# Moving one finish, one scan and one block of transposes at the head of the second up stage

## Chip, cores and metric

The kernel runs on one core of a Trainium2 chip. The metric is the device time of one execution in microseconds (us); the median of four runs before the change is 380.81 us, from 380.46 to 381.58.

## What is computed

The reference is a gated linear attention followed by a feed-forward block with a SoLU activation and a layer norm. All data are float32 on the core.

```python
# attention: batch 4, heads 8, sequence 768, head_dim 48
for t in range(S):
    state = alpha[:, :, t, :, None] * state + einsum('bhd,bhe->bhde', k[:, :, t], v[:, :, t])
    y[:, :, t] = einsum('bhd,bhde->bhe', q[:, :, t], state)
x = y.transpose(0, 2, 1, 3).reshape(3072, 384)
# feed-forward: 384 -> 1024 -> 384
h = x @ w_in
solu = h * softmax(h)
ln = (solu - mean) / sqrt(var + 1e-6) * g_ln
out = ln @ w_out
```

## The kernel before

**Tiling.** The sequence of 768 is cut into six groups of 128 tokens (numbered 0 to 5), each for all four batches. Attention is done in chunked form: within a group, queries and keys are scaled by products of alpha, a masked score matrix is multiplied by the values, and what lies before the group is carried in a state. Scaled queries and keys need running products along the tokens, which VectorE (DVE) makes with scans. The 48 entries of a head are kept as a first 32 and a last 16 (two heads' last entries share a block of 32 rows), so that there are three parts of four blocks each: scan parts 0 and 1 for the first 32 entries, part 2 for the last 16.

**An up stage.** For a group g the loop at the end of `fast_path` (line 891 on) takes the eight pieces f = 0 to 7 of the 1024 hidden columns. `up` issues six matmuls into a PSUM bank h (line 389; there are two such banks), then `up_act`: ScalarE's exponential e (line 403), DVE's product u = h * e (line 404, which frees the bank) and ScalarE's square of u (line 405). `running` (line 420) adds e on GpSimd (POOL) and the square on DVE to running sums, from the second piece on. A `down` stage multiplies u by w_out for one chunk, that is, one batch of a group (line 500), in two halves.

**finish** (lines 511 to 540) closes a chunk. On DVE it issues four instructions: it copies one column of sums (L523), makes two small one-column results (L525, L528), and for group 0 adds a multiple of `mean_sb` to the down result (L533). POOL takes a power (L537), ScalarE scales the row block into `o_sb` (L539), and SyncE (SP) stores it (L540).

**What attention does meanwhile.** While group g is in its up stage, attention of group g+1 is prepared. An order written by hand, the tables `usual` and `first` (lines 828 to 839), names for each piece s what is issued at the head, behind the up, in the middle and at the tail; `attend` (line 841) carries it out. Each engine works in program order. `first` holds for g = 1, the stage which is called the second up here. Names that matter:

- `scan_on(g, i)` (line 229): the forward scan of part i on DVE, aT <- aT, seed (L222). For i = 2 a reciprocal (L233) writes the seeds of all parts first. "on0" and "on1" in the table are parts 0 and 1.
- "lasts" (lines 199 and 251): one DVE transpose of the queries' last 16 entries into qe (L200), and one POOL multiply by scan part 2 (L254).
- "firsts" (lines 196 and 251): one larger DVE transpose into qv (L197), then two POOL multiplies by scan parts 0 and 1 (L254), then the load of the next queries on SP (L141).
- "apart": two ScalarE copies of qe into qv (L247), one for even heads and one for odd.
- "states": the key-value products on TensorE (PE, L364) and four adds to the state on DVE (L374). "v" loads the values on SP (L179). "decay": multiplies of the state on POOL (L263, L264).
- "keys_back": twelve transposes on PE (L300) and three ScalarE copies (kg, L302).
- "scores0" and "scores1": 64 matmuls each into four PSUM banks (L281). "masked0" and "masked1": four DVE products each, which empty those banks into sT (L292). "read0" to "read3" and "values" multiply state and values (L315) into the same four banks.
- "alpha": transposes of alpha and `alpha_over` on ScalarE (L214). `keys` are two POOL multiplies of kT (L243).

**Just ahead of the second up** the program is written out: scans of group 2's alpha backward, `keys_T(2)`, `keys(2)`, load of keys, `scan_on(2, 2)`, `read_values(1)`, `alpha_over(2)`, load of alpha, the rest of `down(3)`, and `finish(3)` (line 824). The loop has a variable `after` (line 899): a chunk in it is finished behind the next piece's `up`.

Of the kernel before, what the change touches and what calls it, by code (L numbers as in the profile page):

```python
# [32 lines left out]
def fast_path(ctx, tc, q, k, v, alpha, moe_w_in, moe_w_out, moe_g_ln, out):  # L33
# [13 lines left out]
    B, H, S, D = q.shape  # L47
# [90 lines left out]
    def load(src, dst, g):  # L138
        t = slice(g * P, (g + 1) * P)
        for b in range(B):  # L140
            nc.sync.dma_start(  # L141
                out=dst[32 * b : 32 * b + 32].rearrange("t h u d -> t h (u d)"),
                in_=src[b, :, t, :].rearrange("h (t u) d -> t h (u d)", u=TQ),
            )
# [65 lines left out]
    def alpha_over(g):  # L210
        x = an.rearrange("p h u d -> p (h u d)")
        sq = one.tile([P, 768], FP, name="sq").bitcast(U8)[:, 0 : x.shape[1]]
        for i, sign in enumerate((1.0, -1.0)):
            nc.scalar.activation(  # L214
                out=sq, in_=x, func=AF.Relu, scale=sign, bias=mone, accum_out=over[:, g, i : i + 1]
            )

    def scan(out, data, start, flip):
        a, o, s = (x.rearrange("p j s -> p (j s)") for x in (data, out, start))
        if flip:  # L220
            a, o, s = a[:, ::-1], o[:, ::-1], s[:, ::-1]
        nc.vector.tensor_tensor_scan(out=o, data0=a, data1=s, initial=1.0, op0=ALU.mult, op1=ALU.add)  # L222
# [6 lines left out]
    def scan_on(g, i):  # L229
        part = slice(NP * i, NP * i + NP)  # L230
        if i == 2:

            nc.vector.reciprocal(out=seed[:, :, 0:1], in_=h4[:, :, 1:2])  # L233
            nc.scalar.copy(out=fend[:, g], in_=h4[:, :, 1])
        scan(aT[:, part], aT[:, part], seed[:, part], False)
# [77 lines left out]
    def y_mm(b, a, r, row, lhsT, rhs, stop=False):  # L313
        begun = reading["begun"]
        nc.tensor.matmul(  # L315
            y_bank(b)[quarter(r), a], lhsT=lhsT, rhs=rhs, start=(b, r) not in begun, stop=stop,
            tile_position=(row, 32 * r), skip_group_check=True,
        )
        begun.add((b, r))
# [23 lines left out]
    def read_values(g, batches=range(B)):  # L343
        if 0 in batches:
            gr[g]["x"] = pair.tile([P, KC, B, P], FP, name="x")
        for b in batches:
            for n, part in enumerate(parts):
                for a, r, h, e in part:
                    y_mm(b, a, r, 0, vn[:, b, h, e], sT[:, b, h], n == len(parts) - 1)
        for b in batches:  # L350
            nc.scalar.copy(out=gr[g]["x"][:, :, b], in_=reading["y"][b])
# [29 lines left out]
    def up(g, f):  # L381
        up_mm(g, f)
        up_act(g, f)
# [110 lines left out]
    def down(n, half, part=slice(0, HF)):  # L494
        g, b = divmod(n, B)
        d = st[n]
        if half == 0 and part.start == 0:
            d["o"] = ps_o.tile([P, 512], FP, tag="o", name="o")
        for f in range(half * HF + part.start, half * HF + part.stop):
            nc.tensor.matmul(  # L500
                d["o"][:, 0 : DM + 1], lhsT=u_of(g, f)[:, b * P : b * P + P], rhs=w_out[:, f], start=(f == 0),
                stop=(f == FC - 1), skip_group_check=True,
            )
# [7 lines left out]
    def finish(n):  # L511
        g, b = divmod(n, B)
        d = st[n]
        s, o = sums[:, n], d["o"][:, 0:DM]
        t0 = b * S + g * P
        if g == G - 1:
            o_sb = work.tile([P, DM], FP, name="o_sb")
            r = gr[g]["r"][:, b : b + 1]
            nc.scalar.activation(out=o_sb, in_=o, func=AF.Copy, scale=r)
            nc.scalar.dma_start(out=out[t0 : t0 + P, :], in_=o_sb)  # L520
            d.clear()
            return
        nc.vector.tensor_copy(out=s[:, 0:1], in_=d["o"][:, DM : DM + 1])  # L523
        t = small.tile([P, 1], FP, name="t")
        nc.vector.scalar_tensor_tensor(  # L525
            out=t, in0=s[:, 0:1], scalar=-1.0 / DFF, in1=s[:, 0:1], op0=ALU.mult, op1=ALU.mult
        )
        nc.vector.tensor_tensor(out=s[:, 3:4], in0=t, in1=gr[g]["s"][:, b : b + 1], op=ALU.add)  # L528
        if g == 0:

            if not d.get("moved"):
                o = work.tile([P, DM + 1], FP, name="o_mean")[:, 0:DM]
            nc.vector.scalar_tensor_tensor(  # L533
                out=o, in0=mean_sb, scalar=s[:, 0:1], in1=d["o"][:, 0:DM], op0=ALU.mult, op1=ALU.add
            )
        r = small.tile([P, 1], FP, name="r")
        nc.gpsimd.tensor_tensor(out=r, in0=s[:, 3:4], in1=mhalf, op=ALU.pow)  # L537
        o_sb = work.tile([P, DM], FP, name="o_sb")
        nc.scalar.activation(out=o_sb, in_=o, func=AF.Copy, scale=r)  # L539
        nc.sync.dma_start(out=out[t0 : t0 + P, :], in_=o_sb)  # L540
        d.clear()
# [272 lines left out]
    for i in range(3):  # L814
# [2 lines left out]
    keys(2)  # L817
    load(k, kn, 3)
    scan_on(2, 2)
    read_values(1)  # L820
    alpha_over(2)
    load(alpha, an, 3)
    down(3, 1, slice(3, HF))
    finish(3)

# [2 lines left out]
        behind={0: "states v keys", 1: "load on2 on0 on1", 2: "lasts firsts", 3: "apart", 5: "decay", 6: "alpha", 7: "back"},  # L830
# [2 lines left out]
    )  # L833
    first = dict(
        head={3: "keys_back", 5: "masked0", 6: "masked1"},
        behind={0: "states v", 1: "on0 on1", 2: "lasts firsts", 3: "apart", 5: "decay", 7: "alpha back"},
        tail={4: "scores0", 5: "scores1", 6: "begin read0 read1"},
        middle={7: "read2 read3 values"},
    )
# [1 line left out]
    def attend(a, what):  # L841

        more = a + 1 < G
        if what == "v":
            load_v(a)
        elif what == "keys":
            keys_T(a)
            keys(a)
            if more:
                load(k, kn, a + 1)  # L850
        elif what[:2] == "on":
            scan_on(a, int(what[2]))
        elif what == "lasts":
            lasts(qn, qe)
            queries(2)
        elif what == "firsts":
            firsts(qn, qv[:, 0:H])
            queries(0)
            queries(1)
            if more:  # L860
                load(q, qn, a + 1)
        elif what == "apart":
            apart()
        elif what == "decay":
            decay(a)
        elif what == "keys_back" and more:
            keys_back(a)
        elif what[:6] == "scores":
            scores(a, int(what[6]))
        elif what[:6] == "masked":  # L870
            masked(int(what[6]))
        elif what == "alpha" and more:
            alpha_T(a + 1)
            alpha_over(a + 1)
        elif what == "load" and more:
            load(alpha, an, a + 1)
        elif what == "back" and more:
            for i in range(3):
                scan_back(a + 1, i)
        elif what == "begin":  # L880
            read_begin()
        elif what[:4] == "read":
            read_state(int(what[4]))
        elif what == "values":
            read_values(a)
        elif what == "states":
            next_state(a - 1)
# [3 lines left out]
    for g in range(1, G + 1):  # L891
        rise, att = g < G, g + 1 < G
        plan = first if g == 1 else usual

        def at(where, s):
            for what in plan[where].get(s, "").split() if att else ():
                attend(g + 1, what)

        after = None
        if not rise:  # L900
            break
        for s in range(FC):
            at("head", s)
            if rise:
                up(g, s)
            if after is not None:
                finish(after)
                after = None
            if s == 0 and g > 1:
                token_sums(g - 1)  # L910
            at("behind", s)
            for f in centres.get(s, ()) if g == 1 else ():
                centre(f)
            if rise and s:
                running(g, s)
            at("middle", s)
            if rise and s == FC - 1:
                todo.append((g * B, 0))
            step = todo.pop(0)
            if step:  # L920
                n, half = step
                down(n, half)
                if half:
                    after = n
            at("tail", s)
        if after is not None:
            finish(after)
        todo = [(n, half) for n in range(g * B, g * B + B) for half in range(2)][1:]
# [492 lines left out]
```

## Time and profile before

| what | value |
| --- | --- |
| median of four runs | 380.81 us (380.46 to 381.58) |
| profiled execution, its own time | 380.86 us |
| its span, first to last instruction | 379.0 us, granted TensorE clock 0.998 |
| PE matmuls busy | 365.9 us |
| VectorE, ScalarE, GpSimd busy | 244.0, 146.9, 128.4 us |
| PE busy in 100 to 120 us, in 120 to 140 us | 18.78, 19.27 us |
| PE busy in each later stretch of 20 or 40 us up to 360 us | all of it |

All times within the execution are microseconds from the start of the span. The profiler's span is 1.86 us shorter than the execution's own time; what lies around it is taken as fixed. A timeline row gives start, length, engine, line of the kernel, operation, output <- inputs, shape and count; what stands in brackets is the time that the engine sat idle before the row and what released it. A row's length runs until its result is written, so the next row of an engine can begin a little before the end of the one ahead of it; it also holds time in which the instruction was started and could not go on. A chain row gives start, length and what the end of the execution waited for at that time. "issue" is time in which the profile shows no wait.

### The profile page before, as it was taken

Reading aid. Unit: us, or ns where it says so; the run is one execution under the profiler, and the core shown is the slowest. Engines: PE = TensorE matmul, PEld = TensorE weight load, DVE = VectorE, ACT = ScalarE, POOL = GpSimd, SP = SyncE. Lnnn points to the kernel's source line nnn. Section 1 sums busy time; section 2 is a strip of 40 time slices with the busy share of each in tenths; the row PEclk is TensorE's granted clock in tenths of the full one; section 3 lists DMA queues with packets and bytes.
Section 4 is the critical chain, followed back from the end, with each engine's and each line's share of the span. In section 5 each row is a group of like instructions: output and inputs, shape, how many; then the busy total and the mean of one; then the engine's idle time right before and its main releaser. Section 6 shows DMA issues by size and latency. Waiting matters only on the chain.

```text
span 379.0 us, 10523 instructions
## 1 busy us (share of the span) xinstructions
PE 365.9 (97%) x4659; PEld 219.8 (58%) x4659; DVE 244.0 (64%) x379; ACT 146.9 (39%) x263; POOL 128.4 (34%) x134
## 2 busy tenths in 40 slices
PE   8789999999898999999999999999999999999995
PEld 8675355566654575555575555675556675555552
DVE  1988879988988876874665874665875411455410
ACT  3628774593455252225351224451233131233111
POOL 5040000042145980662630671630672420333210
PEclk9999999999999999999999999999999999999999
DMA  9983989304096001950002950002400000000011
GB/s 187 192 307 110 222 267 154 85 0 128 24 221 133 3 7 27 186 144 21 22 25 39 202 115 22 23 24 46 62 0 22 22 24 2 22 21 21 22 44 49
DMA packets 65526, 30.78 MB, mean 81 GB/s; under 512 B 47032, under 2 KB 63680, under 8 KB 65472
## 3 DMA queue, kind: packets, MB, share of 16 engines
q1 hardware_dynamic: 64448, 29.10, 34.6%
q10 hardware_dynamic: 1024, 0.92, 0.8%
q8 instruction: 38, 0.62, 0.7%
q14 instruction: 16, 0.13, 0.1%
HBM read 25.30 MB, written 4.72 MB: 79 GB/s over the span
## 4 chain that ended last, share of the span: by engine, by line
PE 71%; DVE 13%; SPq 5%; DMA 5%; ACT 2%; issue 2%; POOL 0%; DVEq 0%
PE o L500 30%; PE h L389 26%; PE y L315 7%; PE a L281 5%; SPq L153 3%; DMA room<-in_moe_w_in_dram 2%; DVE hT L222 2%; DMA out_dram<-o_sb 2%; PE kv L364 1%; DMA an<-in_alpha_dram 1%; DVE sT L292 1%; DVE aT L197 1%; SPq L189 1%; DVE room L404 1%; DVE low L610 1%
## 5 line engine op out<-in xcount | busy, mean ns | idle before, releaser
L500 PE MATMUL o<-w_out,room 128*128 128x385 f32 x384 | 133.8, 491 | 0.0
L389 PE MATMUL h<-x,w_in 128*128 128x512 f32 x288 | 132.4, 599 | 0.6 <-DVE room L404 0.5
L500 PEld LDWEIGHTS o<-w_out,room 128*128 128x128 f32 x384 | 71.2, 190 | 55.8 <-issue 13.1
L389 PEld LDWEIGHTS h<-x,w_in 128*128 128x128 f32 x288 | 52.8, 189 | 59.7 <-issue 48.4
L404 DVE TENSOR_TENSOR room<-h,e 128x512 f32<-128x512 f32 x40 | 27.6, 689 | 81.8 <-ACT e L403 81.7
L403 ACT ACTIVATE e<-h 128x512 f32<-128x512 f32 x40 | 23.9, 598 | 107.4 <-PE h L389 107.4
L420 POOL TENSOR_TENSOR p<-p,e 128x512 f32<-128x512 f32 x30 | 41.9, 1395 | 15.7 <-ACT e L403 15.6
L537 POOL TENSOR_TENSOR r<-sums,mhalf 128x1 f32<-128x1 f32 x20 | 14.9, 746 | 78.6 <-DVE sums L528 78.5
L405 ACT ACTIVATE u<-room 128x512 f32<-128x512 f32 x40 | 25.2, 631 | 36.8 <-DVE room L404 36.8
L292 DVE TENSOR_TENSOR sT<-a,mask 128x512 f32<-128x512 f32 x42 | 26.1, 682 | 8.3 <-PE a L281 8.2
L263 POOL TENSOR_TENSOR state<-state,hT 128x192 f32<-128x192 f32 x20 | 11.3, 582 | 53.4 <-DVE hT L222 53.4
L243 POOL TENSOR_TENSOR kT<-kT,hT 128x1024 f32<-128x1024 f32 (+1 forms) x8 | 14.2, 1792 | 42.0 <-DVE kT L197 33.7
L222 DVE TENSOR_TENSOR_SCAN hT<-aT,unit 128x516 f32<-128x516 f32 x18 | 23.2, 1355 | 7.5 <-ACT aT L683 7.5
L420 DVE TENSOR_TENSOR p<-p,u 128x512 f32<-128x512 f32 x30 | 23.0, 767 | 6.5 <-ACT u L405 6.5
L281 PEld LDWEIGHTS a<-qv,kT 32*128 32x128 f32 x704 | 21.9, 186 | 8.7 <-issue 2.4
L281 PE MATMUL a<-qv,kT 32*128 32x128 f32 x704 | 24.7, 278 | 1.9 <-POOL qv L254 1.1
L222 DVE TENSOR_TENSOR_SCAN aT<-aT,seed 128x516 f32<-128x516 f32 x18 | 26.3, 1493 | 0.2
L315 PE MATMUL y<-sT,vn 128*32 128x128 f32 x768 | 23.6, 274 | 2.7 <-issue 2.3
L315 PEld LDWEIGHTS y<-sT,vn 128*32 128x32 f32 x768 | 20.9, 110 | 4.9 <-issue 3.9
L214 ACT ACTIVATE sq<-an,mone 128x1536 uint8<-128x1536 f32 x12 | 18.9, 1572 | 0.2
L315 PE MATMUL y<-qv,state 32*32 32x128 f32 x960 | 16.7, 277 | 0.0
L539 ACT ACTIVATE o_sb<-o,r 128x384 f32<-128x384 f32 x16 | 9.3, 581 | 18.8 <-POOL r L537 18.8
(146 smaller groups left out, 371.6 us busy)
## 6 DMA issues: line engine op xcount, KB each, us to landing
an<-in_alpha_dram SPq DMA_DIRECT2D x20, 192.0 KB, 4.2
vn<-in_v_dram SPq DMA_DIRECT2D x10, 384.0 KB, 6.2
out_dram<-o_sb SPq DMA_DIRECT2D x20, 192.0 KB, 1.9
room<-in_moe_w_in_dram SPq DMA_DIRECT2D x6, 512.0 KB, 8.5
room<-in_moe_w_out_dram SPq DMA_DIRECT2D x8, 384.0 KB, 4.2
kn<-in_k_dram SPq DMA_DIRECT2D x16, 192.0 KB, 4.6
qn<-in_q_dram SPq DMA_DIRECT2D x16, 192.0 KB, 3.7
kn<-in_k_dram SPq DMA_DIRECT2D x4, 384.0 KB, 5.8
```

What stands on the lines that cost most here:

```text
L214: nc.scalar.activation(out=sq, in_=x, func=AF.Relu, scale=sign, bias=mone, accum_out=over[:, g, i : i + 1])
L222: nc.vector.tensor_tensor_scan(out=o, data0=a, data1=s, initial=1.0, op0=ALU.mult, op1=ALU.add)
L281: nc.tensor.matmul(a[b][:, i], lhsT=kT[quarter(b), kb], rhs=qv[quarter(b), qb], start=kb == h, stop=kb != h, tile_position=(32 * b, 0), sk ...
L292: nc.vector.tensor_tensor(out=sT[:, b, half * NP : half * NP + NP], in0=a[b], in1=mask[:, None, :].to_broadcast([P, NP, P]), op=ALU.mult,)
L315: nc.tensor.matmul(y_bank(b)[quarter(r), a], lhsT=lhsT, rhs=rhs, start=(b, r) not in begun, stop=stop, tile_position=(row, 32 * r), skip_g ...
L389: nc.tensor.matmul(h, lhsT=w_in[:, a, f * P : (f + 1) * P], rhs=d["x"][:, a].rearrange("p b t -> p (b t)"), start=(a == 0), stop=(a == KC ...
L403: nc.scalar.activation(out=e, in_=h, func=AF.Exp)
L404: nc.vector.tensor_tensor(out=u, in0=h, in1=e, op=ALU.mult)
L405: nc.scalar.activation(out=u2, in_=u, func=AF.Square)
L420: eng.tensor_tensor(out=p, in0=d[0][i] if f == 1 else p, in1=d[f][i], op=ALU.add)
L500: nc.tensor.matmul(d["o"][:, 0 : DM + 1], lhsT=u_of(g, f)[:, b * P : b * P + P], rhs=w_out[:, f], start=(f == 0), stop=(f == FC - 1), skip ...
L537: nc.gpsimd.tensor_tensor(out=r, in0=s[:, 3:4], in1=mhalf, op=ALU.pow)
```

## The change

Three edits, all in the order of instructions. `finish(3)` is no longer issued ahead of the loop but, through `after = B - 1`, behind the first piece's `up` of the second up stage. Its place ahead of the loop is not taken; forward scan part 0 of group 2 is issued directly behind part 2 instead of behind the second piece. In `first`, "lasts" moves from behind piece 2 to behind piece 1, ahead of scan part 1; "firsts" stays behind piece 2.

```diff
@@ -817,11 +817,11 @@
     keys(2)
     load(k, kn, 3)
     scan_on(2, 2)
+    scan_on(2, 0)
     read_values(1)
     alpha_over(2)
     load(alpha, an, 3)
     down(3, 1, slice(3, HF))
-    finish(3)
@@ -833,7 +833,7 @@
     first = dict(
         head={3: "keys_back", 5: "masked0", 6: "masked1"},
-        behind={0: "states v", 1: "on0 on1", 2: "lasts firsts", 3: "apart", 5: "decay", 7: "alpha back"},
+        behind={0: "states v", 1: "lasts on1", 2: "firsts", 3: "apart", 5: "decay", 7: "alpha back"},
         tail={4: "scores0", 5: "scores1", 6: "begin read0 read1"},
         middle={7: "read2 read3 values"},
     )
@@ -896,7 +896,7 @@
-        after = None
+        after = B - 1 if g == 1 else None
         if not rise:
             break
```

On DVE the order from scan part 2 on becomes: scan 0, u of piece 0, the finish's four, the four state adds, u of piece 1, lasts, scan 1, the first running sum, u of piece 2, firsts, the second running sum, u of piece 3. Before, it was: the finish's four, u of piece 0, the state adds, u of piece 1, scan 0, scan 1, the first running sum, u of piece 2, lasts, firsts, the second running sum, u of piece 3. On ScalarE the exponential and the square of piece 0 come ahead of `o_sb`, which stays ahead of the exponential of piece 1. On POOL the multiply of qe comes ahead of the first running sum. PE and SP keep their orders.

## Prediction

> **What bounds the kernel now.** The page comes first: who is busy, and for how much of the span.
>
> ```profile
> PE 365.9 (97%) x4659; PEld 219.8 (58%) x4659; DVE 244.0 (64%) x379; ACT 146.9 (39%) x263; POOL 128.4 (34%) x134
> ```
>
> PE sets the time, but its 97% holds stalls inside groups of matmuls. The busy time by stretches of 20 us gives PE 18.78 in 100 to 120, 19.27 in 120 to 140, and all of every stretch from 140 to 360. So this change can gain only before 130 us; what moves PE there moves the end by as much. PE's own timeline of that place, second up, shows it (last columns: length, operation, count, idle time before and its releaser):
>
> ```profile
> 113.71 5.32 PE L389 MATMUL h<-x,w_in 128*128 128x512 f32 x12
> 120.17 0.50 PE L281 MATMUL a<-qv,kT 32*128 32x128 f32 x8 [1.15 <-POOL qv L254]
> 121.01 2.01 PE L281 MATMUL a<-qv,kT 32*128 32x128 f32 x56 [0.33 <-ACT qv L247]
> ...
> 125.72 3.60 PE L281 MATMUL a<-qv,kT 32*128 32x128 f32 x64
> ```
>
> The first scores (L281) wait for the queries, and the second scores take 3.60 where the same 64 matmuls take 2.00 in the chain at 174.08: 1.60 us of hidden wait. The chain that ended last, followed back from there, names what they wait for:
>
> ```profile
> 115.59 1.07 DVE qe L200
> 116.66 1.91 DVE qv L197
> 118.57 0.52 DVE p L420
> 119.09 0.61 DVE room L404
> ...
> 119.72 0.63 ACT u L405
> 120.35 1.22 ACT qv L247 x2
> 121.57 0.49 ACT e L403
> ...
> 123.47 1.36 DVE p L420
> 124.83 2.40 DVE sT L292 x4
> ...
> 127.28 2.05 PE a L281 x58
> ```
>
> Read upwards: the second scores need the banks that masked0 (L292) empties; masked0 stands on DVE behind u4's running sum (p), that behind Square 4, exp 4, the two apart copies (L247), Square 3 and u3 (119.09). I write uN, exp N for chunk N of this up. So the change is worth what it does to u3 and to that last sum.
>
> At the start of the stage ScalarE is late and DVE idles for it. ScalarE's timeline, then DVE's:
>
> ```profile
> 107.84 0.61 ACT L539 ACTIVATE o_sb<-o_mean,r 128x384 f32<-128x384 f32 x1 [2.25 <-POOL r L537]
> 108.36 0.58 ACT L403 ACTIVATE e<-h 128x512 f32<-128x512 f32 x1
> ```
> ```profile
> 103.59 2.40 DVE L222 TENSOR_TENSOR_SCAN aT<-aT,seed 128x516 f32<-128x516 f32 x1
> ...
> 106.07 0.92 DVE L525 SCALAR_TENSOR_TENSOR t<-sums 128x1 f32<-128x1 f32 x1
> ...
> 108.97 0.69 DVE L404 TENSOR_TENSOR room<-h,e 128x512 f32<-128x512 f32 x1 [1.27 <-ACT e L403]
> ```
>
> ScalarE is free at 105.6 (alpha_over's last row, 105.40 + 0.19) but stands 2.25 us before the fourth chunk's o_sb; exp 0 is behind it, though h is ready at about 105.2. DVE then idles 1.27 before u0.
>
> One more thing prices the change. Some DVE operations stretch beside POOL: the scan at 103.59 took 2.40 and the one-column operation at 106.07 took 0.92, against 1.20 for the scan at 160.04 and a median of 0.16 for L525. POOL's two key multiplies run from 102.72 to 104.90 and from 104.86 to 106.97. The scan ends 1.1 after the first one ends, the small operation ends with the second. Operations with two operands in SBUF take turns between the engines. u (L404), which reads h from PSUM, took 0.69 beside POOL too. Who is next when both wait is shown one stage on, in the timelines of DVE and POOL:
>
> ```profile
> 157.87 2.25 DVE L222 TENSOR_TENSOR_SCAN aT<-aT,seed 128x516 f32<-128x516 f32 x1
> 157.16 1.86 POOL L420 TENSOR_TENSOR p<-e 128x512 f32<-128x512 f32 x1
> ```
>
> POOL asked at 157.16, during a scan of 156.72 to 157.87; it ended at 159.02, 1.15 later, and only then did the next scan, queued right behind the first, run. The one that waits gets its turn before the other's next instruction.
>
> **The change, step by step.** No instruction is added or removed; orders change on DVE, ScalarE and POOL, none on PE and SyncE (the listing of both orders). Lengths on DVE are start to start from its timeline: u 0.61 (108.97 to 109.58), four state adds 1.27 (109.58 to 110.85), scan 1.13 (160.04 to 161.16), sum p 0.6, lasts 0.96 and firsts 1.91 (115.51, 116.47, 118.38); the finish's four about 1.05 without POOL.
>
> 1. Scan 0 ahead of u0. DVE is free of scan 2 at 105.9, as now. The second key multiply has waited since 104.86 and takes its turn to 106.97; scan 0 runs to 108.05. It fills the idle 1.27, but 1.05 of that is a wait: the gap is not free room.
> 2. Exp 0 runs at 105.6, u0 at 108.05 (now 108.97). PE's third up waits for u0 now (0.24, row at 109.72); that wait goes, worth nothing by itself, since PE waits at 119 anyway.
> 3. The finish behind it: DVE 108.65 to 109.7, power on POOL 109.25 to 109.80, o_sb 109.83. Exp 1 is still behind o_sb: 110.35, ending 110.93. State adds 109.7 to 110.8. u1 at 110.96, now 110.85. All that step 2 gained is spent here. The store goes out some 2 us later and load_v behind it on SyncE by as much: issued at about 111 instead of 108.95, over 5.0 us as now, landing a median of 6.2 after issue, so by 123; values need it at 138.04: hidden. Nothing else waits there: q's load needs the queries (118.60).
> 4. Lasts a block sooner: 111.57 to 112.7; POOL asks for the qe multiply at about 112.85. Scan 1 is dispatched at 112.54, so it is first, to 113.65; qe (1.18, row at 116.81) then to 114.82, and the sum p of DVE, which is ready at 113.65, waits 1.15 and runs to 115.4. u2 at 115.39, now 114.91: **0.48 later**. Before, no sum met qe, which ran beside the transposes.
> 5. Firsts directly behind u2: 115.99 to 117.90, now 116.47 to 118.38: 0.48 sooner, as 0.96 of lasts is gone from here. The next sum ends at 118.48.
> 6. ScalarE: Square 2 (116.09), three kg copies and exp 3 follow u2 at once now (115.63, 116.16, 117.58), so exp 3 moves with it, to 118.05 to 118.67. u3 needs both and starts at 118.70, now 118.98: **0.28 sooner**. The old order had 0.78 of slack between exp 3's end (118.20) and u3; the new one has none, so exp 3 is what is late next.
> 7. Square 3, apart, exp 4, u4, Square 4: each 0.28 sooner; u4's sum is ready at 123.19 (now 123.47). POOL's two query multiplies end at about 119.65 and 120.8 (now 120.12 and 121.26), its sums at 122.5 and 123.8 (now 122.93 and 124.28). The sum waits for the last of these and starts at 123.8 instead of 124.28. Masked0 starts 0.43 to 0.48 sooner.
> 8. PE: the first scores end with apart, 0.28 sooner; the second with masked0, **0.43 sooner**. Behind them up6, the state reads and masked1 keep their distances: the decay on POOL follows the same sums, and its end (131.18) is 0.84 before the reads (132.02). From there PE has no wait that the chain shows, so the end moves by 0.43. PE's ceiling here is 119.0 to 129.25 less 2.00 + 2.77 + 2.00, or 3.5 us; the change gets an eighth of it.
>
> Sum: 380.86 (the profiled execution's own time, span 379.0) less 0.43 is 380.4. The execution is 0.05 above the median of the four, 380.81; I leave that in the range.
>
> The Trainium skill (SBUF — State Buffer, "Who interferes with whom") says that a DVE instruction with two SBUF inputs contends with a GpSimd instruction that reads SBUF, exclusively, and that the first to issue blocks the other. The rows above (2.40 against 1.20) agree, and it speaks against this change, which moves a scan and a POOL multiply next to each other. Without it, steps 1 and 4 would lose no 1.05 and 1.15, and the estimate would be about 378.7; with it, 380.4. Who is next when both wait that section does not say.
>
> **Rivals.** (a) *The turns fall for the change.* If DVE keeps its turn between scans 2 and 0, all to u3 is some 0.75 sooner (u1 is then bound by exp 1 behind o_sb); if scan 1's sum goes ahead of qe, u2 is 1.15 sooner. Either gives 0.43 + 0.75 or 0.43 + 1.15, so 379.7 to 379.3, both together 378.5. Against it: the pair at 157. For it: only one form of meeting is shown there.
>
> (b) *The turns fall against it: slower.* The place is scan 1 and qe. If qe's multiply gets its turn before scan 1 (it decides when lasts' result reaches POOL less than 0.3 us, step 4's margin, ahead of my dates, or when DVE's dispatch is that late), then qe ends at 114.0, scan 1 at 115.1, POOL's own sum, waiting since 114.0, at 116.25, and DVE's sum at 116.85. u2 is 1.9 later than now, exp 3 ends at 120.1 and u3 starts 1.15 later than now. With 0.15 given back at the sums the end is 1.0 later: 381.9.
>
> (c) *Nothing moves.* The order listing shows that exp 0 does pass the finish, so the edit does what it says; but if u4's sum meets another POOL sum, the 0.43 becomes 0 to 0.2: 380.7.
>
> **Chances.** About 0.2% (0.76 us) is what a measurement of this kernel can tell from no change: faster is below 380.05, slower above 381.57. The forecast has 0.45 and (c) 0.13, both within; (a) 0.28; (b) 0.14. For 8 in 10 the range takes in (a) to 379.3 and most of (b), to 381.6.
>
> **What would show it.** In the profile of after: scan 0 stretched to about 2.1 beside the key multiply; u0 at 108.0; u1 near 111; DVE's first sum stretched to about 1.75 with qe in front; u2 later than 114.91; no idle DVE between exp 3 and u3; second scores of 3.5 ending near 128.9. Wrong if scan 0 ends by 107.1 or u2 comes before 114.5 (a), if scan 1 ends after 115 (b), or if PE waits anew behind 130 us.

## The result and the profile after

The changed kernel takes 380.25 us (median of 52 runs, 379.38 to 381.44), the kernel before 381.0 (median of 78 runs in all, 380.09 to 383.28). The ratio is 0.9976, with a 95% interval of 0.9970 to 0.9982: 0.75 us by the medians, 0.7 to 1.1 us by the interval. The forecast was 380.4, 0.43 us faster; 380.25 lies inside its range of 379.3 to 381.6 and on the side that was forecast. The gain came out larger: by the ratio 0.24%, past the 0.2% that the forecast named as its border, though 380.25 is not below the 380.05 that was named with it.

The profiled execution of after took 380.70 us with a span of 378.8, against 380.86 and 379.0. That is 0.2 us, less than the medians show; the section on the hardware tells where the rest of this one execution went. PE's timeline of after at the same place as before:

```profile
119.52 0.50 PE L281 MATMUL a<-qv,kT 32*128 32x128 f32 x8 [0.74 <-POOL qv L254]
120.55 2.01 PE L281 MATMUL a<-qv,kT 32*128 32x128 f32 x56 [0.52 <-ACT qv L247]
...
125.26 3.42 PE L281 MATMUL a<-qv,kT 32*128 32x128 f32 x64
```

The same three rows stood at 120.17, 121.01 and 125.72. The waits are still there; their sum is little smaller (0.74 + 0.52 against 1.15 + 0.33), but everything stands earlier. The chain that ended last, followed back, now runs:

```profile
113.76 1.52 DVE p L420
115.28 0.61 DVE room L404
...
116.45 1.54 ACT kg L302 x3
118.00 0.51 ACT e L403
...
118.53 0.70 DVE room L404
...
123.01 1.18 DVE p L420
124.19 2.40 DVE sT L292 x4
```

Before, DVE's transposes (lasts, firsts) led to u3; now the first running sum, u2, ScalarE's kg copies and exp 3 do. The sum takes 1.52 of the chain's time for what is 0.6 of work. (Further back both chains name a DMA, ahead of the first sum in before and ahead of lasts in after. DVE's rows there follow each other without idle time, so that DMA held nothing up.) The head of the stage, ScalarE's timeline of after:

```profile
105.59 0.58 ACT L403 ACTIVATE e<-h 128x512 f32<-128x512 f32 x1
...
109.88 0.62 ACT L539 ACTIVATE o_sb<-o_mean,r 128x384 f32<-128x384 f32 x1 [0.45 <-POOL r L537]
110.40 0.58 ACT L403 ACTIVATE e<-h 128x512 f32<-128x512 f32 x1
```

Exp 0 is 2.77 us earlier (108.36 before), exp 1 is not (110.24 before). DVE's timeline, and then the two rows of POOL that belong to it:

```profile
103.72 4.46 DVE L222 TENSOR_TENSOR_SCAN aT<-aT,seed 128x516 f32<-128x516 f32 x2
108.10 0.66 DVE L404 TENSOR_TENSOR room<-h,e 128x512 f32<-128x512 f32 x1
...
113.67 1.61 DVE L420 TENSOR_TENSOR p<-u,u 128x512 f32<-128x512 f32 x1
115.20 0.68 DVE L404 TENSOR_TENSOR room<-h,e 128x512 f32<-128x512 f32 x1
```
```profile
112.92 1.81 POOL L254 TENSOR_TENSOR qe<-qe,aT 128x512 f32<-128x512 f32 x1 [3.08 <-ACT e L403]
114.70 1.74 POOL L420 TENSOR_TENSOR p<-e 128x512 f32<-128x512 f32 x1
```

Two scans that take 1.2 each when nothing is in their way took 4.46 beside POOL's key multiplies. The multiply of qe, 1.19 before, took 1.81, because it asked during scan 1; the sum behind scan 1 then took 1.61, and POOL's own sum behind qe 1.74, where it took 1.30 before.

### The profile page after: what moved, and what is told of

The parts are those of the page before. It is cut to its first block, busy times and chain, and to the rows that moved or that the text cites. A ratio compares the mean times of both kernels' runs of the same rounds, so it can differ in the third digit from the quotient of the medians.

```text
span 378.8 us, 10523 instructions
## 1 busy us (share of the span) xinstructions
PE 366.8 (97%) x4659; PEld 220.3 (58%) x4659; DVE 244.1 (64%) x379; ACT 146.7 (39%) x263; POOL 129.5 (34%) x134
## 4 chain that ended last, share of the span: by engine, by line
PE 73%; DVE 14%; ACT 7%; issue 3%; DMA 2%; SPq 0%; ACTq 0%; DVEq 0%
PE o L500 30%; PE h L389 24%; PE y L315 8%; PE a L281 5%; DVE hT L222 3%; PE warm L445 2%; DVE room L404 2%; DVE sT L292 1%; DMA an<-in_alpha_dram 1%; ACT sq L586 1%; DVE aT L197 1%; PE kv L364 1%; PE tp L300 1%; DVE top L602 1%; DVE aT L222 1%
```

## Experiments

To compare executions that begin a little differently, the table counts dates from the start of scan 2 (103.59 in before, 103.72 in after), in us. "PE" is the first matmul of piece 6's up, right behind the second scores. Before and after were each profiled twice; both values stand where they differ.

| kernel | u0 | u1 | u2 | exp 3 | u3 | masked0 | PE | PE against before |
| --- | --- | --- | --- | --- | --- | --- | --- | --- |
| before | 5.39, 5.38 | 7.26 | 11.33, 11.32 | 14.00, 13.99 | 15.39, 15.37 | 21.16, 21.17 | 25.67 | |
| after, forecast | 4.46 | 7.37 | 11.80 | 14.46 | 15.11 | 20.73 | 25.24 | -0.43 |
| after | 4.38, 4.39 | 7.29, 7.30 | 11.49, 11.53 | 14.16, 14.19 | 14.81, 14.85 | 20.40, 20.45 | 24.90, 24.95 | -0.77, -0.72 |
| e1 finish only | 2.58 | 6.61 | 10.66 | 13.33 | 14.73 | 20.50 | 25.00 | -0.67 |
| e2 scan 0 only | 6.70 | 8.58 | 11.52 | 14.28 | 15.64 | 21.39 | 25.89 | +0.22 |
| e3 lasts only | 5.38 | 7.25 | 13.64 | 16.30 | 16.96 | 22.54 | 27.04 | +1.37 |
| e4 scan 1 first | 4.36 | 7.26 | 10.53 | 13.20 | 13.85 | 19.50 | 24.00 | -1.67 |
| e5 finish late | 4.35 | 6.49 | 10.68 | 13.35 | 14.00 | 19.76 | 24.26 | -1.41 |
| e6 both | 4.36 | 6.60 | 9.89 | 12.60 | 13.26 | 18.84 | 23.34 | -2.33 |
| e7 no qe multiply | 4.38 | 7.29 | 10.55 | 13.23 | 13.88 | 19.46 | 23.96 | -1.71 |
| e8 scan 1 in the gap | 4.40 | 7.18 | 9.39 | 12.49 | 13.12 | 18.21 | 22.72 | -2.95 |

The two profiled executions of before, and the two of after, agree within 0.05 us in every column, so a single profile is taken to tell differences of 0.1 us here, which times with intervals of 0.5 to 1.4 us can't.

My theory, TURNS, says that the end follows u3 and the sum ahead of masked0, and that DVE and POOL, taking turns at operations with two operands in SBUF, set those. Its rivals: QUERIES (what counts is that the last 16 are turned sooner), SUM OF PARTS (each edit gives about a third), and later EARLY EXPONENTIAL (only exp 0 and u0 ahead of the finish count).

### One edit alone

**e1, the finish moved, nothing else.**

```diff
     down(3, 1, slice(3, HF))
-    finish(3)
...
-        after = None
+        after = B - 1 if g == 1 else None
```

> Only the finish is moved behind the second up's first piece; scan 0 and the queries' last 16 stay where they were. Three theories. TURNS (mine): the end follows u3 and the sum ahead of masked0, and DVE's and POOL's turns set those. Then this edit alone brings u0 to 106.2, the state adds to 107.9, u1 to 110.05 (exp 1, now bound by PE's h at 109.4; before 110.85), and u2, u3 and masked0 each 0.8 us sooner than before: 0.8 us faster, ratio 0.998, no worse than the whole change. QUERIES: PE's first wait names the queries, so what counts is that the last 16 are turned sooner; this edit alone gives 0 to 0.2 us. SUM OF PARTS: each of the three edits gives about a third of what the change gave (0.75 us), so 0.25 us here.

Measured: 380.24 us against 381.06, ratio 0.9986 (0.9970 to 1.0003). The times alone don't settle it, the dates do: PE 0.67 us sooner, nearly all that the whole change gives. DVE's timeline of e1:

```profile
105.95 0.69 DVE L404 TENSOR_TENSOR room<-h,e 128x512 f32<-128x512 f32 x1 [0.18 <-ACT e L403]
...
109.98 0.69 DVE L404 TENSOR_TENSOR room<-h,e 128x512 f32<-128x512 f32 x1 [1.30 <-ACT e L403]
```

u0 stands where it was expected, and the idle time is not gone: 1.30 us of it moved to u1, which waits for exp 1 and that for PE's h. QUERIES (0 to 0.2 expected) and SUM OF PARTS (0.25) fall by the dates. The gain is had another way than in the whole change: in e1 u1 is 0.65 sooner and u3 follows u2 by 4.07 as before (4.06); in the change u1 is no sooner and u3 follows u2 by 3.32.

**e2, scan 0 ahead, nothing else.**

```diff
     scan_on(2, 2)
+    scan_on(2, 0)
...
-        behind={0: "states v", 1: "on0 on1", 2: "lasts firsts", ...},
+        behind={0: "states v", 1: "on1", 2: "lasts firsts", ...},
```

> Only scan 0 is moved, directly behind scan 2 and ahead of the finish, which stays ahead of the first piece. TURNS: scan 0 waits for the second key multiply to 107.0 and ends at 108.05, the finish ends at 109.1 on DVE, o_sb at 109.75, exp 0 and u0 at 110.2 (before 108.97), u1 at 112.1 (before 110.85), scan 1 behind a POOL sum to 114.4, u2 at 115.0 (before 114.91): within 0.2 us of before. QUERIES: 0. SUM OF PARTS: 0.25 us faster.

Measured: 380.95 us against 381.06, ratio 0.9997 (0.9983 to 1.0011). The dates follow the expectation: u0 1.3 later, u1 1.3 later, u2 0.2, PE 0.22 later. Alone the scan stands in the way of the finish and of exp 0. SUM OF PARTS (0.25 faster) falls by the dates.

**e3, lasts a block sooner, nothing else.**

```diff
-        behind={0: "states v", 1: "on0 on1", 2: "lasts firsts", ...},
+        behind={0: "states v", 1: "lasts on0 on1", 2: "firsts", ...},
```

> Only the queries' last 16 are turned one piece sooner; scans 0 and 1 follow them, the finish stays. TURNS: on DVE scan 0, scan 1 and the first sum now each meet a POOL multiply or sum that waits (qe, then POOL's own first sum): scan 0 to 113.6, qe to 114.7, scan 1 to 115.8, POOL's sum to 116.9, DVE's sum to 117.5, u2 at 117.45 instead of 114.91, exp 3 at 120.1, u3 at 120.8 instead of 118.98: 1.8 us slower, ratio 1.0047. QUERIES: faster by 0.5 to 1 us, since qe and qv come sooner. SUM OF PARTS: 0.25 us faster.

Measured: 382.48 us against 381.06, ratio 1.0038 (1.0024 to 1.0051): 1.4 us slower, by the dates 1.37. DVE's timeline of e3, then POOL's:

```profile
112.54 3.24 DVE L222 TENSOR_TENSOR_SCAN aT<-aT,seed 128x516 f32<-128x516 f32 x2
115.70 1.72 DVE L420 TENSOR_TENSOR p<-u,u 128x512 f32<-128x512 f32 x1
117.34 0.68 DVE L404 TENSOR_TENSOR room<-h,e 128x512 f32<-128x512 f32 x1
```
```profile
112.87 1.82 POOL L254 TENSOR_TENSOR qe<-qe,aT 128x512 f32<-128x512 f32 x1 [4.95 <-DVE qe L200]
114.65 2.21 POOL L420 TENSOR_TENSOR p<-e 128x512 f32<-128x512 f32 x1
```

Five operations of two engines (scan, qe, scan, POOL's sum, DVE's sum) stand in one file: the first takes 1.16 as if alone, each of the others is longer than alone, and their rows end one behind the other, at 113.70, 114.69, 115.78, 116.86 and 117.42. QUERIES and SUM OF PARTS both expected a gain here; both fall. The three edits alone give -0.67, +0.22 and +1.37 by the dates, together -0.75: they don't add up. The rows of e3 point to why: scan 0 stands in the file there, and in the change it is out of the way. No kernel with two of the three edits was run, so what each pair gives is not shown.

### What the turns cost

**e4, scan 1 ahead of lasts.**

```diff
-        behind={..., 1: "lasts on1", 2: "firsts", ...},
+        behind={..., 1: "on1 lasts", 2: "firsts", ...},
```

> The whole change, but scan 1 stands ahead of the turning of the last 16 instead of behind it. TURNS: the first sum then runs before POOL's qe multiply asks, at 113.6, and does not wait; u2 at 114.25 to 114.3 (change: 115.20), exp 3 at 117.0, u3 at 117.6 (change: 118.53), masked0 some 0.9 us sooner than in the change: 0.9 us faster than the change, 1.6 to 1.7 us faster than before, ratio 0.9955. QUERIES: the last 16 come 1.1 us later again, so slower than the change by up to 1 us. SUM OF PARTS: the third part is mostly undone, ratio 0.9982.

Measured: 379.10 us against 381.06, ratio 0.9950 (0.9933 to 0.9968). The dates put it 0.9 us ahead of the change, as expected. DVE's timeline of e4:

```profile
111.17 1.22 DVE L222 TENSOR_TENSOR_SCAN aT<-aT,seed 128x516 f32<-128x516 f32 x1
...
113.24 0.68 DVE L420 TENSOR_TENSOR p<-u,u 128x512 f32<-128x512 f32 x1
113.84 0.67 DVE L404 TENSOR_TENSOR room<-h,e 128x512 f32<-128x512 f32 x1
```

POOL's row of e4:

```profile
113.56 1.40 POOL L254 TENSOR_TENSOR qe<-qe,aT 128x512 f32<-128x512 f32 x1 [4.17 <-DVE qe L200]
```

The sum is issued 0.32 before POOL's qe and takes 0.68 instead of 1.61. Lasts come 1.1 us later than in the change (9.01 against 7.90 from scan 2's start), and the kernel is faster: QUERIES and SUM OF PARTS, which expected it slower than the change, fall.

**e7, the qe multiply left out.** For group 2 the last 16 of the queries are not scaled.

```diff
             lasts(qn, qe)
-            queries(2)
+            if a != 2:
+                queries(2)
```

> The whole change with POOL's multiply of qe left out for group 2 (the last 16 of its queries are not scaled); DVE still turns them and apart still copies them. It takes away the turn that the first sum waits for. TURNS: the first sum runs at 113.67 without a wait (0.66 long instead of 1.61), u2 at 114.25 (change: 115.20), u3 at 117.6, masked0 0.9 us sooner: 0.9 us faster than the change, ratio to before 0.9952, the same as with scan 1 ahead of the turning. If the sum's stretch is not POOL's turn but some other slowing of DVE, it stays near 1.6 and the ratio near 0.9976.

Measured: 379.19 us against 381.35, ratio 0.9944 (0.9931 to 0.9957); u2 at 10.55 and PE at 23.96, as in e4. The sum, DVE's timeline of e7:

```profile
113.12 0.66 DVE L420 TENSOR_TENSOR p<-u,u 128x512 f32<-128x512 f32 x1
```

Taking POOL's multiply away takes the stretch away, with DVE's order unchanged. The stretch is POOL's turn.

### Where the finish should stand

**e5, the finish behind piece 6.**

```diff
-            if after is not None:
+            if after is not None and (g > 1 or s == 6):
                 finish(after)
```

> The whole change, but the fourth chunk's finish goes behind piece 6 instead of piece 0, where DVE idles 1.06 us ahead of u6. TURNS: the finish's 1.0 us on DVE and o_sb leave the chain to u3; u1 is bound by exp 1 behind Square 0 and starts at 109.9 to 110.0 (change: 111.0), and u2, u3 and masked0 come 1.0 us sooner than in the change: 1.0 us faster than the change, ratio to before 0.995. EARLY EXPONENTIAL (a rival: only exp 0 and u0 ahead of the finish count, and they stay where they are): as the change, 0.9976.

Measured: 379.25 us against 381.35, ratio 0.9944 (0.9931 to 0.9956). By the dates it is 0.66 ahead of the change, by the two ratios 1.2 with intervals 0.5 apart (1.0 expected). Of the dates, u1, u2 and u3 come 0.8 sooner and not 1.0, as exp 1 waits for PE's h (ScalarE's row below), and masked0 0.65, as the sum ahead of it takes 1.36 where it took 1.18 in the change. Against before the times give 2.1 us (1.7 to 2.6) and the dates 1.41; what makes the rest is not shown.

```profile
109.66 0.60 ACT L403 ACTIVATE e<-h 128x512 f32<-128x512 f32 x1 [0.19 <-PE h L389]
```

EARLY EXPONENTIAL falls: u0 stands where it stood and the kernel is faster.

**e6, both.** The edits of e4 and e5 together.

> The finish behind piece 6 and scan 1 ahead of the turning of the last 16, together. TURNS: u1 at 109.9, scan 1 at 110.5, the turning at 111.6, the first sum at 112.6 just ahead of qe's multiply (asked at 112.9), u2 at 113.2, exp 3 at 115.9 (PE's h for piece 3 ready at 115.8), u3 at 116.45 (change: 118.53); masked0 at about 121.5 (change: 124.12): 2.1 to 2.6 us faster than the change, ratio 0.991 to 0.992. If instead PE's fourth and fifth up or the apart copies bind first, 1.5 us, ratio 0.9935. EARLY EXPONENTIAL: 0.9952, as with scan 1 first alone.

Measured: 378.54 us against 381.35, ratio 0.9929 (0.9915 to 0.9944). The dates put it 1.6 ahead of the change, so the 2.1 to 2.6 that TURNS expected first did not come. The 1.5 named beside it did in size, but not by what it named: u1 waits for exp 1 and that for PE's h, which makes u1 and u2 0.4 and u3 0.5 later than expected (all counted from scan 2's start), and the sum ahead of masked0 still met POOL's, so masked0 gained what u3 did, 1.55, and no more. ScalarE's row of exp 1 in e6, then DVE's of that sum:

```profile
109.08 0.60 ACT L403 ACTIVATE e<-h 128x512 f32<-128x512 f32 x1 [0.28 <-PE h L389]
```
```profile
120.84 1.18 DVE L420 TENSOR_TENSOR p<-p,u 128x512 f32<-128x512 f32 x1 [0.70 <-ACT u L405]
```

EARLY EXPONENTIAL expected no more than e4's gain; the dates are 0.66 ahead of e4's.

**e8, scan 1 ahead of u1.** DVE idles 0.52 there in e6.

```diff
-        behind={0: "states v", 1: "on1 lasts", 2: "firsts", ...},
+        behind={0: "states v on1", 1: "lasts", 2: "firsts", ...},
```

> The finish behind piece 6 as in the kernel with both, and scan 1 now ahead of u1, where DVE idles 0.52 us for exp 1, instead of behind it. TURNS: u1 0.5 us later, which nothing waits for, the first sum and u2 0.5 us sooner (12.4 against 113.0 less 100); exp 3 then waits for PE's own h of piece 3 (ready 13.4 us after the second up's first matmul) and not for the kg copies, so u3 gains 0.3 us and no more: 0.3 us faster than the kernel with both, ratio 0.992. EARLY EXPONENTIAL: no difference.

(The 12.4 and 113.0 there mean 112.4 and 113.0 of the span.) Measured: 378.41 us against 381.33, ratio 0.9919 (0.9903 to 0.9935), the fastest kernel of this study; against e6 the times don't tell (the intervals overlap). Its dates are 0.62 ahead of e6's. u2 gained the 0.5, and the chain that ended last now goes through PE's own h, as expected:

```profile
113.17 2.59 PE h L389 x6
...
115.85 0.61 ACT e L403
...
116.48 0.70 DVE room L404
...
120.96 0.69 DVE p L420
```

u3 gained only 0.14. That masked0 gained 0.63 was not expected: the sum ahead of it (last line) has its turn without a wait here, 0.69 against 1.18 in e6, because POOL's sums come 0.65 sooner, counted from scan 2's start, and u4 0.13.

### The two kernels once more

> The changed kernel once more, for a second profile. TURNS: counted from scan 2's start, u2 at 11.5, u3 at 14.8, masked0 at 20.4 us, as in the first profile, within 0.1; ratio 0.9976. What differs between executions is the gap in PE's values matmuls near 197 us, 0 to 0.7 us.

> The kernel before once more, for a second profile. TURNS: counted from scan 2's start, u2 at 11.3, u3 at 15.4, masked0 at 21.2 us, as in the first profile, within 0.1; ratio 1. The gap in PE's values matmuls near 197 us is 0 to 0.7 us here too.

Measured: 380.53 us, ratio 0.9972 (0.9958 to 0.9986), and 381.27 us, ratio 0.9999 (0.9988 to 1.0011). All dates agree with the first profiles within 0.05. The two profiled executions of after differ by 0.94 us all the same (380.70 and 381.64); 0.62 of that lies ahead of scan 2 (103.72 and 104.34), 0.3 in the gaps told below, so those gaps are not all that differs.

## Why the prediction was right, and where its size was off

**What bounds the kernel** was right: the gain was had before 130 us, and PE's distances behind piece 6's up are the same within 0.1 us in all twelve profiles but for the gaps told below. Of the 3.5 us that step 8 gave as the ceiling, e8 got 2.95.

**Steps 1 to 3** held to 0.08 us. Scan 0 waited for the key multiply, u0 came at 4.38 (4.46 forecast), and u1 came no sooner than before: the 1.27 of idle time were not free room, and the finish that left the front of exp 0 went to the front of exp 1. e5 shows the price of that place: without it u1 is 0.8 sooner.

**Step 4** was right in its order (scan 1, qe, the sum) and too large in its terms. From scan 1's dispatch to u2 it reckoned 1.11 + 1.15 + 0.6, or 2.85; the rows give 2.61 (112.59 to 115.20). Its terms were lengths of operations that start alone. In the file qe's row ends at 114.73, 0.97 after scan 1's (113.76), where it takes 1.19 by itself, and the sum's ends 0.55 later at 115.28, where it takes 0.66. Why is not shown: part of a row may be start-up, which passes during the wait, or an operation may give up its turn before its row ends. With the 0.08 of steps 1 to 3, u2 was 0.16 to 0.2 late, not 0.48.

**Steps 5 and 6** held: with lasts out from between u2 and u3, u3 follows u2 by 3.32 to 3.37 in the change and in e3 to e7 (4.06 to 4.12 in before, e1 and e2). The slack of exp 3 is gone, the kg copies and exp 3 follow u2 by 2.67 (2.66 forecast), u3 starts as exp 3 ends. With u2 0.3 sooner than reckoned, u3 gained 0.55 instead of 0.28. **Steps 7 and 8** carried that through: masked0 and PE 0.75 sooner instead of 0.43, which is what the medians show (0.75). The term that was mis-sized is the wait in step 4 (2.85 from scan 1 to u2, measured 2.61): 0.24 of the 0.32 us by which u2 came sooner than forecast.

**The rivals.** Rival (a) didn't happen: scan 0 did not keep DVE's turn (4.46 for two scans) and the sum did not pass qe (1.61). Its price for the second of these, 1.15, was too high, as step 4's wait was: e4 lets the sum pass qe by order and gets 0.9, and e7 takes the meeting away and gets the same. With both of its turns the rival gave 378.5; the 378.7 that the prediction gives for no turns at all does not follow from its steps, and nothing else rests on it. Rival (b)'s meeting, POOL's own sum ahead of DVE's, is what e3 shows, by another way: 1.4 us slower. Rival (c) falls by the dates.

**The Trainium skill** (SBUF — State Buffer, "Who interferes with whom") says that a DVE instruction with two SBUF inputs contends with a GpSimd instruction that reads SBUF. It was the rule that spoke against this change, and the runs agree: lasts sooner costs 1.37 us alone (e3), and the meeting of qe and the first sum 0.9 us within the change (e4, e7).

## What to carry to other kernels

An idle stretch on one engine is not free room when a second engine's operation already stands waiting for the same turn: look up what the other engine holds at that date, and put a moved operation where the other has nothing to ask. When a producer (here the transpose into qe) is moved forward, the consumer that it releases on the other engine moves too, so put the operations that must not meet it ahead of the producer: one swap of two entries of the table (e4) gave more than the three edits of the change. And a gain at the front of a chain is spent at the next thing the moved work stands in front of; work that nobody waits for, like this finish, belongs where its engine idles and nothing critical is queued behind it (e5).

## What the runs showed of the hardware

**Turns of DVE and POOL.** In all cases in this stage where both waited, they alternated, whichever way the programs were ordered: four in a file in the change (scan 1, qe, DVE's sum, POOL's sum), five in e3. An operation that reads one operand from PSUM was not stretched in this stage: u took 0.66 to 0.72 in all twelve profiles, masked0's four 2.47 or 2.48, beside POOL or not.

**Gaps in PE's stream of short matmuls.** The 128 values matmuls of a group take 3.70 us at best and up to 0.8 more, in the second up (near 138) and in the next one (near 195), in before and after alike, and differently in each execution. PE's timeline of before, and then of e4, at the same place of the program:

```profile
194.75 3.70 PE L315 MATMUL y<-sT,vn 128*32 128x128 f32 x128
```
```profile
192.99 2.83 PE L315 MATMUL y<-sT,vn 128*32 128x128 f32 x95
196.21 1.14 PE L315 MATMUL y<-sT,vn 128*32 128x128 f32 x33 [0.40 <-issue]
```

Nothing that the profile shows is waited for ("issue"). In the next up the instruction queue starts a 16 KB load 0.2 to 0.4 us behind the first of these matmuls. In the three profiles where that load took 0.95 to 1.03 us (before, e5, e6) there is no gap; in the other nine it took 1.15 to 1.45 us, with gaps of 0.22 to 0.69. That they belong together is argued from this, not shown; in the second up the load's length alone does not order the gaps (0.88 us goes with 0.45 in after and with 0.82 in e3).

These gaps and the start of scan 2 are why the profiled execution of after kept only 0.2 of its 0.75 us: it has such a gap of 0.34 ahead of 197.19 where before has none, one 0.18 larger near 139, and scan 2 began 0.13 later. The first profile of before had the smallest gaps of the twelve. Single times of one kernel differ by up to a microsecond and more where the dates of the stage agree to 0.05.
